# Leaky unit of a mixture layer: one scaled copy on ScalarE and one maximum on VectorE in place of two VectorE operations

## The chip, the cores and the metric

The kernel runs on one core of one Trainium2 chip. Its engines are TensorE (PE, matmuls; its weight loads are PEld), VectorE (DVE), ScalarE (ACT), GpSimd (POOL) and SyncE (SP), which issues nearly all transfers here. The metric is the device time in microseconds, the median of several runs. Each engine works through its own queue in order; semaphores order the engines among each other.

## The reference

Windowed attention (2 batches, 8 heads, 768 positions, head size 64; each query sees its last 96 positions and the first 8), then two expert layers over the 1536 tokens, both 512 to 2048 to 512:

```python
def _moe_ref(x, w_in, w_out, alpha):
    h = x @ w_in
    g = np.maximum(h, 0.0) + alpha * np.minimum(h, 0.0)
    return (g @ w_out).astype(np.float32)

def _moe2_ref(x, w_in, w_out, a, b):
    h = x @ w_in
    P = a[0] + a[1]*h + a[2]*h*h + a[3]*h*h*h
    Q = 1.0 + abs(b[0])*abs(h) + abs(b[1])*h*h
    return ((P / (Q + 1e-06)) @ w_out).astype(np.float32)
```

alpha is one number for each of the 2048 hidden columns, between 0 and about 1.26, so some are above 1.

## The kernel before

Every matmul operand is split into a high half (float32r) and a low half (the rest), and a product is made of three passes: high by high, high by low, low by high. The hidden layer is worked in 16 chunks of 128 columns (fc) for each of three groups (g) of 512 tokens, for each of the two layers: 96 steps in all, 48 leaky and 48 rational. For each step, `first` (L738) does the 12 matmuls of L745 into one PSUM bank, the unit turns the bank into the halves ghi and glo, and `second` (L798) does the 12 matmuls of L811 from them into banks 4 to 7. In a leaky step the unit is `leaky` (L748): L751 makes alpha * min(h, 0) in the tile act, L752 adds max(h, 0) to it in the bank, L753 casts the bank to ghi on ScalarE, and the returned function, called later, subtracts (L754) into glo.

The order of work is written by hand (manual_schedule), so each engine's queue has the order of the program. There are three stretches. First, attention alone (`alone`, L575, units u of two z steps). Second, 16 joint slots (`joint_slot`, L855, s = 0 to 15, u = 10 + s): each has the scores and the values of attention, one leaky step and parts of the weight work. Third, plain slots (`plain_slot`, L876), where the leaky step of slot s is that of the first() before it and second() works two steps behind.

A joint slot runs in this order: `opening(u)` (scores, reciprocal, row minima L452, low halves of the q or k cast before, `values` L512 and L514 for earlier units, exponentials L459, the casts to xhi and xlo, L524 and L525); one `tick`; `first(s)`; another `tick`; `turning(u)` (transposes of the probabilities and of the next q or k block, `copy_p` L497 or L499, and the q or k cast L412 or L409 on ScalarE); `leaky(s)`; the low halves of q or k (L413, L410); the low half of the leaky unit; `second(s - 1)`. In the joint stretch every `first(s)` writes bank 3, so `first(s + 1)` has to wait until L754 of slot s has read it. `values` writes bank 2, which the q or k cast and its low half read before.

A `tick` (L284) moves weight loading on: `tick` casts a joined weight tile to its high half (L302 on ScalarE), subtracts for the low half (L305 on VectorE), joins the two words of the next tile (L314, L315, L316 on VectorE) and scales the one after (L325 on ScalarE). L302 waits for L316 of the tick before.

`moe_constants` (L183) issues the transfers of alpha and of the coefficients in unit u = 2; `moe_constants_ready` (L189) makes constants from the coefficients on GpSimd and ScalarE in u = 6.

Of the kernel before, what the change touches and what calls it, by code (L numbers as in the profile page):

```python
# [8 lines left out]
F32 = mybir.dt.float32  # L9
# [3 lines left out]
AF = mybir.ActivationFunctionType  # L13
ALU = mybir.AluOpType
# [3 lines left out]
P = 128  # L18
# [7 lines left out]
NF = DFF // P  # L26
# [34 lines left out]
class Kernel:  # L61
# [52 lines left out]
    def small_consts(self):  # L114
        const = self.small
        self.ni = const.tile([P, 4], I32, name="ni")
        self.nf = const.tile([P, 4], F32, name="nf")
        self.neg = const.tile([P, 4], F32, name="neg")
        self.nv = const.tile([P, 2], F32, name="nv")
        self.fl = const.tile([P, 3], F32, name="fl")  # L120
        self.fi = const.tile([P, 1], I32, name="fi")
        self.al = const.tile([P, NF], F32, name="al")
        self.co = const.tile([P, 6], F32, name="co")
        self.na = const.tile([P, 4], F32, name="na")
        self.ab = const.tile([P, 2], F32, name="abs_b")
        self.cq = const.tile([P, 1], F32, name="cq")
        const.tile([P, 16], F32, name="pad")
# [61 lines left out]
    def moe_constants_ready(self):  # L189
        nc, co = self.nc, self.co  # L190
        nc.gpsimd.tensor_scalar(self.na, co[:, 0:4], -1.0, 1.0, ALU.mult, ALU.mult)
        nc.scalar.activation(self.ab, co[:, 4:6], AF.Abs)
        nc.gpsimd.memset(self.cq, 1.0 + 1e-6)

    def load_tokens(self, nm, i, tile, heads=slice(0, H)):
        b, qb = divmod(i, NB)
        src = {"q": self.q, "k": self.k, "v": self.v}[nm][b, heads, qb * P : (qb + 1) * P, :]
        self.nc.sync.dma_start(out=tile[:, heads], in_=src.rearrange("h s d -> s h d"))
# [532 lines left out]
    def moe(self):  # L731
        nc, steps, banks = self.nc, self.steps, self.banks
# [15 lines left out]
        def leaky(n):  # L748
            fc, h = steps[n][2], hbank.pop(n)
            t, hi, lo = self.act[n % 2], self.ghi[n % 2], self.glo[n % 2]  # L750
            nc.vector.tensor_scalar(t, h, 0.0, self.al[:, fc : fc + 1], ALU.min, ALU.mult)  # L751
            nc.vector.scalar_tensor_tensor(h, h, 0.0, t, ALU.max, ALU.add)  # L752
            nc.scalar.copy(hi, h)  # L753
            return lambda: nc.vector.tensor_sub(lo, h, hi.bitcast(F32))  # L754

        def rational_parts(n):
            p = flat[NST - 2 + n % 2]
# [97 lines left out]
        def joint_slot(s, halves):  # L855
            u = JOIN // 2 + s
            opening, turning = halves or (lambda u: None, lambda u: ())
            if s >= CH + 2 and s < CH + 2 + NEARLY:
                self.reload(s - CH - 2)
            opening(u)  # L860
            if s:
                self.tick(True, 2 * s - 1 in self.starts)
            first(s)
            self.tick(True, 2 * s in self.starts)
            lows = turning(u)
            low = leaky(s)
            for more in lows:
                more()
            low()
            if s:  # L870
                second(s - 1)
            if s == LATE - 1:
                self.tick(True, 2 * s + 1 in self.starts)
                self.spill()

        def plain_slot(s):  # L876
# [22 lines left out]
            if late >= LATE and steps[late][0]:  # L899
                rational_e(late)  # L900
            low = leaky(early) if ready and not steps[early][0] else None
            self.tick(True, 2 * s in self.starts)
            if low:
# [87 lines left out]
```

## Time and profile before

| | us |
|---|---|
| median of 3 runs (lowest, highest) | 651.09 (649.98, 651.37) |
| span of the profiled execution | 646.6 |
| TensorE busy | 619.1 (96%) |
| VectorE busy | 537.8 (83%) |
| ScalarE busy | 378.1 (58%) |
| GpSimd busy | 128.2 (20%) |

The profile is that of one execution; its own time outside the span is not given. Busy shares are means over stretches with different limits, so the table by stretch and the chain of waits tell more than the shares do. Durations of matmuls are modelled at their ends. An instruction that starts before the one ahead of it on its engine has ended overlaps with it.

### The profile page before, as it was taken

The numbers are of one execution on the slowest core, as the hardware profiler recorded it, in microseconds if no ns is written. First come the engines' busy times: TensorE is split into PE (matmuls) and PEld (weight loads), VectorE is DVE, ScalarE is ACT, GpSimd is POOL, SyncE is SP. The second block draws the span as 40 slices with busy tenths as digits, with TensorE's granted clock in tenths as the row PEclk, the third lists the DMA queues.
The fourth block names the chain that finished last, engine by engine and source line by source line (L and its number), as shares of the span: only waits on it lengthen the run. The fifth ranks groups of instructions, "written<-read, shape, count | busy, mean of one in ns | idle before, by whom it ended". The sixth has DMA issues, their size and how long they took to land.

```text
span 646.6 us, 9486 instructions
## 1 busy us (share of the span) xinstructions
PE 619.1 (96%) x3234; PEld 506.9 (78%) x3234; DVE 537.8 (83%) x1015; ACT 378.1 (58%) x787; POOL 128.2 (20%) x204
## 2 busy tenths in 40 slices
PE   7878999999999999999999999999999999999995
PEld 6756877778878888888888878887788888888783
DVE  5686899977658878958879989999989997786985
ACT  4886666676534323324333377777687776766672
POOL 4574222122210000000000013212222222222221
PEclk7799998999999999999999999999999999999998
DMA  8998798879788933412612600231111000400302
GB/s 159 196 272 224 205 285 261 250 257 278 241 280 261 368 90 90 123 60 65 196 33 66 195 2 2 65 98 32 38 60 33 1 1 0 131 2 0 131 0 71
DMA packets 84858, 82.81 MB, mean 128 GB/s; under 512 B 45312, under 2 KB 61952, under 8 KB 84800
## 3 DMA queue, kind: packets, MB, share of 16 engines
q1 hardware_dynamic: 84656, 81.98, 42.8%
q8 instruction: 27, 0.44, 0.3%
q14 instruction: 31, 0.25, 0.1%
q10 hardware_dynamic: 144, 0.13, 0.1%
HBM read 60.21 MB, written 19.92 MB: 124 GB/s over the span
## 4 chain that ended last, share of the span: by engine, by line
PE 66%; DVE 21%; ACT 7%; POOL 2%; issue 2%; DMA 1%; SPq 0%; ACTq 0%; POOLq 0%; DVEq 0%
PE bank L811 32%; PE bank L745 31%; DVE dx L315 3%; ACT prob L459 3%; DVE dx L316 3%; DVE prob L452 2%; DVE dx L314 1%; DVE bank L752 1%; DVE glo L754 1%; DVE act L751 1%; ACT ghi L753 1%; POOL prob L471 1%; DVE act L789 1%; DVE stage L788 1%; DVE stage L787 1%
## 5 line engine op out<-in xcount | busy, mean ns | idle before, releaser
L796 POOL TENSOR_TENSOR glo<-act,ghi 128x512 fp32r<-128x512 f32 (+1 forms) x49 | 67.2, 1372 | 385.1 <-ACT ghi L792 363.9
L753 ACT CAST ghi<-bank 128x512 fp32r<-128x512 f32 x48 | 28.2, 588 | 111.7 <-DVE bank L752 90.3
L745 PE MATMUL bank<-xhi,winhi_f 128*128 128x512 f32 x256 | 68.4, 389 | 0.0
L745 PE MATMUL bank<-xhi,winlo_f 128*128 128x512 f32 x256 | 68.4, 389 | 0.0
L745 PE MATMUL bank<-xlo,winhi_f 128*128 128x512 f32 x256 | 68.4, 389 | 0.0
L471 POOL TENSOR_SCALAR prob<-prob,rec 128x232 f32<-128x232 f32 (+1 forms) x96 | 44.4, 481 | 99.2 <-DVE rec L477 70.6
L459 ACT ACTIVATE prob<-prob,stat 128x232 f32<-128x232 f32 (+1 forms) x96 | 45.0, 475 | 23.6 <-DVE stat L452 23.6
L745 PEld LDWEIGHTS bank<-xlo,winhi_f 128*128 128x128 f32 x256 | 48.1, 188 | 10.0
L745 PEld LDWEIGHTS bank<-xhi,winhi_f 128*128 128x128 f32 x256 | 48.1, 188 | 10.0
L745 PEld LDWEIGHTS bank<-xhi,winlo_f 128*128 128x128 f32 x256 | 48.0, 188 | 10.0
L315 DVE SCALAR_TENSOR_TENSOR dx<-de,dx 128x512 int32<-128x512 int32 x64 | 50.8, 794 | 2.2
L754 DVE TENSOR_TENSOR glo<-bank,ghi 128x512 fp32r<-128x512 f32 x48 | 33.0, 688 | 17.4 <-ACT ghi L753 10.7
L316 DVE SCALAR_TENSOR_TENSOR dx<-stage,dx 128x512 int32<-128x512 int32 x64 | 45.7, 714 | 2.2
L751 DVE TENSOR_SCALAR act<-bank,al 128x512 f32<-128x512 f32 x48 | 35.8, 745 | 12.6 <-PE bank L745 12.6
L792 ACT CAST ghi<-act 128x512 fp32r<-128x512 f32 (+1 forms) x49 | 30.1, 615 | 26.3 <-DVE act L789 26.3
L763 ACT ACTIVATE stage<-bank 128x512 f32<-128x512 f32 (+1 forms) x49 | 28.9, 589 | 27.3 <-PE bank L745 27.1
L772 DVE SCALAR_TENSOR_TENSOR stage<-stage,abs_b 128x512 f32<-128x512 f32 (+1 forms) x49 | 36.0, 737 | 10.5 <-ACT stage L764 10.5
L325 ACT ACTIVATE de<-stage 128x512 f32<-128x512 f32 x64 | 43.0, 676 | 0.6 <-DMA stage<-in_moe_w_out_dram 0.6
L811 PE MATMUL bank<-wouthi_f,ghi 128*128 128x512 f32 x144 | 41.5, 393 | 1.3 <-ACT ghi L792 1.3
L811 PE MATMUL bank<-wouthi_f,glo 128*128 128x512 f32 x144 | 41.3, 392 | 0.0
L811 PE MATMUL bank<-woutlo_f,ghi 128*128 128x512 f32 x144 | 41.0, 389 | 0.0
L787 DVE SCALAR_TENSOR_TENSOR stage<-stage,cq,bank 128x512 f32<-128x512 f32 (+1 forms) x49 | 35.9, 734 | 3.3 <-ACT bank L777 3.2
(204 smaller groups left out, 1443.1 us busy)
## 6 DMA issues: line engine op xcount, KB each, us to landing
stage<-in_moe_w_in_dram SPq DMA_DIRECT2D x32, 512.0 KB
stage<-in_moe_w_out_dram SPq DMA_DIRECT2D x32, 512.0 KB
part<-saved_f SPq DMA_DIRECT2D x16, 256.0 KB
va<-in_v_dram SPq DMA_DIRECT2D x13, 256.0 KB
saved_f<-part SPq DMA_DIRECT2D x12, 256.0 KB
out_dram<-part SPq DMA_DIRECT2D x11, 256.0 KB
rawk<-in_k_dram SPq DMA_DIRECT2D x10, 256.0 KB
rawq<-in_q_dram SPq DMA_DIRECT2D x10, 256.0 KB
```

Source lines behind the costliest of these rows:

```text
L315: lambda: nc.vector.scalar_tensor_tensor(y, e, -(2**31), y, ALU.bitwise_and, ALU.bitwise_or),
L316: lambda: nc.vector.scalar_tensor_tensor(y, low, 29, y, ALU.logical_shift_right, ALU.bitwise_or),
L325: nc.scalar.mul(self.de[n % 2], self.staged(n)[:, :, :, 1].bitcast(F32), 2.0**-112)
L459: nc.scalar.activation(p[:, j - e, :w], p[:, j - e, :w], AF.Exp, bias=st[:, j : j + 1], scale=-1.0, accum_out=st[:, 4 + j : 5 + j],)
L471: nc.gpsimd.tensor_scalar(p[:, j, :w], p[:, j, :w], r[:, e + j : e + j + 1], 1.0, ALU.mult, ALU.mult)
L745: nc.tensor.matmul(bk, w["in", a][:, c, :], x[:, c, :], start=e == 0, stop=e == len(seq) - 1)
L751: nc.vector.tensor_scalar(t, h, 0.0, self.al[:, fc : fc + 1], ALU.min, ALU.mult)
L754: return lambda: nc.vector.tensor_sub(lo, h, hi.bitcast(F32))
L772: nc.vector.scalar_tensor_tensor(w, w, self.ab[:, 0:1], ab, ALU.add, ALU.mult)
L787: nc.vector.scalar_tensor_tensor(w, w, self.cq[:, 0:1], r, ALU.add, ALU.mult)
L796: nc.gpsimd.tensor_tensor(lo, u, hi.bitcast(F32), ALU.subtract)
L811: nc.tensor.matmul(y[d], lhs, rhs, start=begin and e == 0, stop=last and e == 2)
```

## The change

The leaky unit is written as a maximum. Where alpha is at most 1, max(h, 0) + alpha * min(h, 0) is max(h, alpha * h); where it is above 1 it is the minimum of the two, which is minus the maximum of -h and -alpha * h. So each hidden column has a sign sg (1 or -1) and sa = sg * alpha. ScalarE writes sa * h to act, VectorE writes max(sg * h, act) to the bank, which is then sg times the result; the sign is taken back in the two halves: ScalarE makes ghi from sg times the bank, VectorE glo from sg times the bank less ghi. sg and sa are made once, by three GpSimd operations on 128x16.

```diff
+        self.sg = const.tile([P, NF], F32, name="sg")
+        self.sa = const.tile([P, NF], F32, name="sa")
...
         nc.gpsimd.memset(self.cq, 1.0 + 1e-6)
+        nc.gpsimd.tensor_scalar(self.sg, self.al, 1.0, 2.0, ALU.is_le, ALU.mult)
+        nc.gpsimd.tensor_scalar(self.sg, self.sg, 1.0, 1.0, ALU.subtract, ALU.mult)
+        nc.gpsimd.tensor_tensor(self.sa, self.sg, self.al, ALU.mult)
...
         def leaky(n):
             fc, h = steps[n][2], hbank.pop(n)
             t, hi, lo = self.act[n % 2], self.ghi[n % 2], self.glo[n % 2]
-            nc.vector.tensor_scalar(t, h, 0.0, self.al[:, fc : fc + 1], ALU.min, ALU.mult)
-            nc.vector.scalar_tensor_tensor(h, h, 0.0, t, ALU.max, ALU.add)
-            nc.scalar.copy(hi, h)
-            return lambda: nc.vector.tensor_sub(lo, h, hi.bitcast(F32))
+            sg, sa = self.sg[:, fc : fc + 1], self.sa[:, fc : fc + 1]
+            nc.scalar.activation(t, h, AF.Copy, scale=sa)
+            nc.vector.scalar_tensor_tensor(h, h, sg, t, ALU.mult, ALU.max)
+            nc.scalar.activation(hi, h, AF.Copy, scale=sg)
+            return lambda: nc.vector.scalar_tensor_tensor(lo, h, sg, hi.bitcast(F32), ALU.mult, ALU.subtract)
```

## Rows read from the trace of the kernel before

**Rows 1.** Table by stretch: us, busy (instructions) of each engine, PE clock, DMA share, GB/s.
```profile
56.00:132.00 76.00, 71.74 (x504) 58.28 (x505) 65.92 (x167) 48.95 (x132) 15.23 (x41) 0.98 0.85 245
132.00:186.00 54.00, 53.37 (x371) 43.34 (x370) 39.73 (x102) 33.45 (x91) 12.90 (x32) 1.00 0.80 251
186.00:378.00 192.00, 192.00 (x863) 158.84 (x862) 155.23 (x249) 68.42 (x119) 0.00 (x0) 1.00 0.45 143
```
**Rows 2.** Timeline of VectorE in slot 1: start, duration, instruction, idle before it.
```profile
69.79 0.75 DVE L751 TENSOR_SCALAR act<-bank,al 128x512 f32<-128x512 f32 x1
70.57 0.70 DVE L752 SCALAR_TENSOR_TENSOR bank<-bank,act 128x512 f32<-128x512 f32 x1
...
71.92 0.69 DVE L754 TENSOR_TENSOR glo<-bank,ghi 128x512 fp32r<-128x512 f32 x1
```
**Rows 3.** Timeline of ScalarE at the end of slot 0.
```profile
61.42 0.64 ACT L412 ACTIVATE qhi<-bank 128x512 fp32r<-128x512 f32 x1
61.91 0.63 ACT L753 CAST ghi<-bank 128x512 fp32r<-128x512 f32 x1
```
**Rows 4.** Timelines of VectorE and TensorE at the end of slot 0.
```profile
62.09 0.69 DVE L413 SCALAR_TENSOR_TENSOR qlo<-bank,qhi 128x512 fp32r<-128x512 f32 x1 [1.59 <-ACT qhi L412]
62.70 0.68 DVE L754 TENSOR_TENSOR glo<-bank,ghi 128x512 fp32r<-128x512 f32 x1
...
62.84 0.44 PE L512 MATMUL bank<-pt,va 128*64 128x128 f32 x4 [0.30 <-DVE qlo L413]
```
**Rows 5.** Groups of instructions by form: shapes, count, busy us, mean ns, idle before.
```profile
L768 ACT ACTIVATE act<-bank,na 128x512 f32<-128x512 f32 x47 | 37.0, 787 | 0.0
...
L783 DVE SCALAR_TENSOR_TENSOR act<-act,na,bank 128x512 f32<-128x512 f32 x47 | 35.1, 747 | 1.7
...
L764 ACT ACTIVATE stage<-bank,abs_b 128x512 f32<-128x512 f32 x47 | 32.3, 687 | 0.0
L788 DVE SCALAR_TENSOR_TENSOR stage<-stage,bank 128x512 f32<-128x512 f32 x47 | 32.3, 687 | 1.6
...
L763 ACT ACTIVATE stage<-bank 128x512 f32<-128x512 f32 x47 | 28.1, 597 | 27.3 <-PE bank L745 27.1
```
**Rows 6.** Timeline of ScalarE: the leaky unit's cast in slots 1, 2, 3, 7.
```profile
71.31 0.59 ACT L753 CAST ghi<-bank 128x512 fp32r<-128x512 f32 x1 [0.53 <-DVE bank L752]
...
80.90 0.59 ACT L753 CAST ghi<-bank 128x512 fp32r<-128x512 f32 x1 [1.12 <-DVE bank L752]
...
90.39 0.59 ACT L753 CAST ghi<-bank 128x512 fp32r<-128x512 f32 x1 [1.57 <-DVE bank L752]
...
129.44 0.59 ACT L753 CAST ghi<-bank 128x512 fp32r<-128x512 f32 x1 [1.70 <-DVE bank L752]
```
**Rows 7.** Timeline of TensorE: the waits that end slots 7 and 13.
```profile
130.04 0.44 PE L512 MATMUL bank<-pt,va 128*64 128x128 f32 x4 [0.77 <-DVE klo L410]
...
183.04 1.19 PE L745 MATMUL bank<-xhi,winhi__119 128*128 128x512 f32 x4 [0.63 <-DVE glo L754]
```
**Rows 8.** TensorE's wait that ends slot 4, then three windows of 2 us.
```profile
100.76 0.66 PE L512 MATMUL bank<-pt,va 128*64 128x128 f32 x8 [1.51 <-DVE qlo L413]
...
100.00:102.00 2.00, 1.14 (x9) 0.90 (x10) 1.94 (x7) 0.65 (x2) 0.29 (x1) 0.88 1.03 378
102.00:104.00 2.00, 2.00 (x6) 1.52 (x6) 1.52 (x8) 2.00 (x8) 1.47 (x4) 0.50 1.13 328
104.00:106.00 2.00, 2.00 (x9) 1.56 (x8) 1.93 (x4) 1.29 (x4) 0.33 (x1) 0.77 0.56 200
```
**Rows 9.** Timelines of GpSimd and VectorE in unit u = 6.
```profile
36.71 0.50 POOL L476 TENSOR_SCALAR rec<-stat 128x4 f32<-128x4 f32 x1
...
38.34 0.17 DVE L477 RECIPROCAL rec<-rec 128x4 f32<-128x4 f32 x1
```
**Rows 10.** A plain slot: ScalarE's timeline, and TensorE's block from the chain.
```profile
225.47 0.59 ACT L753 CAST ghi<-bank 128x512 fp32r<-128x512 f32 x1 [2.22 <-PE bank L811]
...
223.58 2.72 PE bank L811 x12
```

## The prediction

> **What bounds the kernel now.** I read the page first: TensorE is busy for 96% of the span. That is an average, so the table by stage comes next [rows 1]. From 186 to 378 us TensorE has no idle time at all, and there VectorE and ScalarE can change freely. From 132 to 186 us it lacks 0.6 us of 54. From 56 to 132 us, the stretch in which attention and the first expert layer share the engines (slots 0 to 8 of joint_slot), it lacks 4.3 us of 76 while VectorE is busy for 65.9 of 76. So I followed the chain of waits there, slot by slot, in the timelines. In every slot VectorE runs straight through: weight joins L314 to L316, then the leaky unit L751, L752 and L754 [rows 2], then the row minima of the next scores. TensorE waits for it, not the other way round: values() waits for the low half of q or k (L410, L413), which stands in VectorE's queue right behind L752. From slot 0 to slot 7 the end is set by this VectorE chain; from slot 8 by TensorE.
>
> The question is therefore not how busy ScalarE is, but when it is free inside a joint slot. There it has copy_p and the q or k cast ahead of the leaky unit in its queue, and both engines set out from the same event: the weight cast L302 of ScalarE waits for the join L316 of VectorE, so a late VectorE also makes ScalarE late.
>
> **Part 1: durations.** Taken out is L751: L752 starts 0.78 us after it [rows 2]. Added is one ScalarE pass over 128x512 from a bank into act with a per-partition scale. The nearest rows are L763 (no per-partition operand) 0.597, L764 (one) 0.687, L768 (two) 0.787 us [rows 5]. I take 0.69, since L764 has the same shape, source and one such operand; the ends are 0.60 and 0.79. The cast L753 becomes the same kind of pass: 0.59 [rows 3, 6] to 0.69, so 0.10 more, with ends 0 and 0.20. L752 gets a per-partition scalar: 0.70 [rows 2] to 0.755, by the step from L788 (0.687, none) to L783 (0.747, one) [rows 5]. The subtraction L754 becomes the same form: 0.69 to 0.74. Low ends for these two: no change.
>
> **Part 2: one joint slot.** Let W be ScalarE's wait for VectorE ahead of its cast L753 [rows 6]. It is the only hole that the new pass can use. The pass may start 0.10 before the end of the instruction ahead of it (L753 starts 0.15 before the end of L412 in slot 0 [rows 3]), lasts 0.69, and the hand-over takes 0.04. So the maximum can start W - 0.63 before the old start of the cast; the old L752 started 0.74 before it (70.57 and 71.31 [rows 2, 6]). Its shift is 1.37 - W, and never better than -0.78. Behind it the maximum lasts 0.06 longer, the cast 0.10, the subtraction 0.05. VectorE leaves the slot 1.58 - W later than now:
> - slot 0: its cast has W = 0 and starts at 61.91 as soon as L412 is through [rows 3]; L751 and L752 were done by then, under the wait for qhi of 1.59 us [rows 4]. Now: pass 61.91 to 62.60, maximum 62.64 to 63.40, cast 63.42 to 64.11, subtraction from 64.13, not from 62.70 [rows 4]: +1.43 at its start, +1.48 at its end. qlo (62.09 [rows 4]) is queued behind the maximum and moves to 63.3; values(), which waited for it at 62.84 [rows 4], moves by 1.2. A chain of four hand-overs, three of them on the path, now stands where two were hidden.
> - slot 1, W = 0.53: +1.05.
> - slots 2, 5 and 6, W = 1.12, 1.12 and 1.14 (one row stands for three): +0.46, +0.46, +0.44.
> - slots 3 and 4, W = 1.57 and 1.55 (one row for both; here the probabilities have half the width and copy_p is shorter): +0.01, +0.03.
>
> Sum to the end of slot 6: 3.93 us. In slot 7, W = 1.70, and what TensorE waits for is klo behind the maximum (0.77 us [rows 7]): 1.37 - 1.70 + 0.06 = -0.27. That leaves +3.66 for TensorE at first(8). From there TensorE has no gap until 183.04, where it waits 0.63 us for L754 [rows 7]. In slots 8 to 13 the pass fits into longer waits of ScalarE, VectorE runs 0.1 to 0.5 us ahead of its present place in each, and this wait goes: -0.63. Late next is TensorE itself. Result of the joint stretch: **+3.03 us**.
>
> **Part 3: the other 32 leaky steps.** From 186 us on the pass costs nothing: in plain_slot the cast even waits for TensorE to give back its buffer (2.22 us, at 225.47 [rows 10]), and between that release and the matmuls that read the halves lie three blocks of 12 matmuls of 2.72 us each [rows 10], over 8 us; the new chain of four is about 2.9 us long. TensorE goes on without a gap, so nothing that VectorE saves here (0.6 us a step) reaches the end. If that cover were gone, a step would cost the same 1.58 - W.
>
> **Part 4: the three GpSimd operations** stand in moe_constants_ready, ahead of L476 in GpSimd's queue. They also make GpSimd wait for alpha there, whose transfer was issued ahead of that of the coefficients which GpSimd uses at that point without a wait. L476 runs from 36.71 for 0.50 us; VectorE reads its result at 38.34, since it is busy until then [rows 9]. Cover: 1.1 us. Three operations of 0.2 to 0.5 us take 0.6 to 1.5: I count 0, the bound is +0.4.
>
> **Sum.** The profiled execution spans 646.6 us; the median of the runs is 651.09, so 4.5 us lie around the span, and I leave them as they are. 651.1 + 3.0 = **654.1 us**. Low end (no cost for a per-partition operand on either engine): slot 0 +1.18, the others 1.27 - W, so 1.18 + 0.74 + 0.15 - 0.30 - 0.28 + 0.15 + 0.13 = 1.77, slot 7 -0.43, the wait -0.63: +0.7, 651.8. High end (two steps of 0.1 for each ScalarE pass): 1.68 + 1.25 + 0.66 + 0.21 + 0.23 + 0.66 + 0.64 = 5.33, slot 7 -0.17, -0.63: +4.5, 655.6.
>
> **Rivals.** A, the sum above: 0.55.
>
> B, the per-partition operands cost nothing, for instance because they are fetched while the instruction waits. Against it: L764 and L768 differ from L763 in step. 651.8, chance 0.15.
>
> C, the clock of TensorE. After a wait of 1.51 us that ends slot 4 the granted clock was 0.88, 0.50 and 0.77 in three windows of 2 us [rows 8], which is the lower of its levels (1.2 of 2.4 GHz) for part of them: 2 x (0.12 + 0.50 + 0.23) = 1.7 us lost. It costs nothing there, since VectorE is later still. The change adds waits in slots 0, 2, 5 and 6. If the fall comes at slot 8 or later, where TensorE sets the end, it counts: 654.1 + 1.7 = 655.8, chance 0.15.
>
> D, faster: VectorE's load decides. If ScalarE had the copy ready before VectorE arrives in slots 1 to 7, each would give -0.78 + 0.06 + 0.10 + 0.05 = -0.57; seven of them with the +1.48 of slot 0 make -2.5, 648.6, and TensorE has room for it (the 4.3 us that it lacks up to 132 us [rows 1]). It sets in above W = 1.58 and is full at W = 2.15. Slots 1 to 6 lie between 0.53 and 1.57, so the rows speak against it, but W was set by a chain that changes too: 0.15. The Trainium skill, Perfetto Trace Analysis, section "Optimizing Scalar/DVE Operations", says that where the vector engine is saturated, offloading some of its work to the scalar engine may make sense; by that rule alone the result would be D. The trace agrees on the saturation (65.9 of 76 us) and not on the place: the scalar engine is free elsewhere in the slot.
>
> Against the move speaks a rule of the Trainium skill, ScalarE: Activation LUTs, "Rules for kernel authors": max, min, add and mul belong on the vector engine. The rows here put the pass on the scalar engine slightly below the one taken out (0.687 against about 0.75), so it is not the duration that costs. By the rule, with 0.75 or more for the pass, slots 0 to 6 would add 0.06 each, 0.4 in all: 654.5.
>
> **How the numbers follow.** A run tells apart about 0.2%, 1.3 us: 649.8 to 652.4 is no change. A and C are slower (0.70), B the same (0.15), D faster (0.15). The range takes in B, the bounds of A and C, and leaves out D: 651.6 to 656.2.
>
> **What the profile after would show.** Right: L753's place in slot 0 about 1.5 us later, VectorE idle ahead of the maximum in slots 0 to 2 with ScalarE's pass as releaser, first matmuls of slot 3 about 3 us later and of slot 8 some 3.5 us later, the 0.63 us wait at slot 14 gone, and from 190 us on the same order as before, shifted. Wrong: a pass of 0.6 us (B), half clock after slot 7 (C), no idle VectorE ahead of the maximum (D), or GpSimd late with L476 by more than 1.1 us (then up to 0.4 more).

## The result and the profile after

| | kernel before | changed kernel |
|---|---|---|
| median of 4 runs, us (lowest, highest) | 650.54 (648.47, 651.37) | 653.38 (653.13, 654.77) |
| span of the profiled execution, us | 646.6 | 651.4 |

The ratio is 1.0063, with a 95% interval of 1.0045 to 1.0081: 2.84 us slower, where +3.03 was forecast. The two spans are 4.8 us apart, which is not the size of the effect. The profiled execution of after has its own time, 653.13, so 1.73 us lie around its span; with as much around it, the profiled execution of before took about 648.3, near the lowest of its runs.

The table by stretch of the changed kernel answers to [rows 1] (us, busy and instructions of TensorE, its weight loads, VectorE, ScalarE and GpSimd, then granted clock, DMA share and GB/s):

```profile
56.00:132.00 76.00, 68.92 (x466) 56.28 (x467) 57.41 (x148) 52.10 (x136) 14.94 (x40) 0.96 0.79 227
132.00:186.00 54.00, 53.35 (x379) 43.41 (x378) 39.38 (x105) 39.22 (x102) 11.72 (x30) 1.00 0.78 252
186.00:378.00 192.00, 192.00 (x874) 158.60 (x873) 135.40 (x216) 93.62 (x155) 2.27 (x4) 1.00 0.47 151
```

The change does what it says: from 186 to 378 us VectorE is busy 20 us less (155.2 before) and ScalarE 25 us more (68.4 before), and TensorE has no gap in either. From 56 to 132 us VectorE is less busy too, 57.4 for 65.9 us, and yet TensorE lacks 7.1 us there where it lacked 4.3 (0.7 us of it because first(0) begins at 56.70 and not at 55.94). VectorE was relieved of work and came later. The end of slot 0 shows how, first ScalarE's timeline and then VectorE's, which answer to [rows 3, 4] (start, duration, instruction, idle before it and what released it):

```profile
62.16 0.64 ACT L417 ACTIVATE qhi<-bank 128x512 fp32r<-128x512 f32 x1
62.65 0.73 ACT L757 ACTIVATE act<-bank,sa 128x512 f32<-128x512 f32 x1
64.20 0.69 ACT L759 ACTIVATE ghi<-bank,sg 128x512 fp32r<-128x512 f32 x1 [0.83 <-DVE bank L758]
```
```profile
63.41 0.76 DVE L758 SCALAR_TENSOR_TENSOR bank<-bank,sg,act 128x512 f32<-128x512 f32 x1 [6.44 <-ACT act L757]
64.08 0.68 DVE L418 SCALAR_TENSOR_TENSOR qlo<-bank,qhi 128x512 fp32r<-128x512 f32 x1
64.92 0.75 DVE L760 SCALAR_TENSOR_TENSOR glo<-bank,sg,ghi 128x512 fp32r<-128x512 f32 x1 [0.16 <-ACT ghi L759]
```

VectorE has nothing to do for 6.44 us and then gets the scaled copy only behind the q cast, at 63.38. Before the change it did the two operations of the leaky unit inside that hole:

```profile
59.01 0.75 DVE L751 TENSOR_SCALAR act<-bank,al 128x512 f32<-128x512 f32 x1 [2.80 <-PE bank L745]
59.80 0.70 DVE L752 SCALAR_TENSOR_TENSOR bank<-bank,act 128x512 f32<-128x512 f32 x1
```

The steps now follow each other in single file: pass, maximum, cast, subtraction. In the following slots the same wait stands ahead of the maximum, between 0.3 and 1.5 us; VectorE in slots 1, 2, 3 and 7:

```profile
74.57 0.76 DVE L758 SCALAR_TENSOR_TENSOR bank<-bank,sg,act 128x512 f32<-128x512 f32 x1 [1.52 <-ACT act L757]
...
84.51 0.76 DVE L758 SCALAR_TENSOR_TENSOR bank<-bank,sg,act 128x512 f32<-128x512 f32 x1 [0.91 <-ACT act L757]
...
94.01 0.76 DVE L758 SCALAR_TENSOR_TENSOR bank<-bank,sg,act 128x512 f32<-128x512 f32 x1 [0.47 <-ACT act L757]
...
133.81 0.76 DVE L758 SCALAR_TENSOR_TENSOR bank<-bank,sg,act 128x512 f32<-128x512 f32 x1 [0.34 <-ACT act L757]
```

The groups of the four instructions on the page of the changed kernel (count, busy us, mean ns, idle before) answer to [rows 2, 5]:

```profile
L758 DVE SCALAR_TENSOR_TENSOR bank<-bank,sg,act 128x512 f32<-128x512 f32 x48 | 36.4, 758 | 41.6 <-ACT act L757 41.5
L759 ACT ACTIVATE ghi<-bank,sg 128x512 fp32r<-128x512 f32 x48 | 33.0, 688 | 50.5 <-DVE bank L758 35.4
L760 DVE SCALAR_TENSOR_TENSOR glo<-bank,sg,ghi 128x512 fp32r<-128x512 f32 x48 | 35.9, 749 | 22.4 <-PE bank L817 14.3
L757 ACT ACTIVATE act<-bank,sa 128x512 f32<-128x512 f32 x48 | 33.2, 691 | 27.2 <-PE bank L750 27.2
```

### The profile page after: what moved, and what is told of

It reads as the page before. It is cut to its first block, busy times and chain, and to the rows that moved or that the text cites. A ratio compares the mean times of both kernels' runs of the same rounds, so it can differ in the third digit from the quotient of the medians.

```text
span 651.4 us, 9519 instructions
## 1 busy us (share of the span) xinstructions
PE 622.4 (96%) x3234; PEld 509.9 (78%) x3234; DVE 510.1 (78%) x967; ACT 412.6 (63%) x835; POOL 129.1 (20%) x207
## 4 chain that ended last, share of the span: by engine, by line
PE 76%; DVE 12%; ACT 6%; POOL 1%; issue 1%; DMA 1%; SPq 1%; ACTq 0%; DVEq 0%; POOLq 0%
PE bank L817 35%; PE bank L750 35%; DVE dx L320 2%; PE bank L442 1%; PE bank L407 1%; PE bank L517 1%; ACT prob L464 1%; DVE prob L457 1%; DVE dx L321 1%; POOL prob L476 1%; ACT pt L504 1%; PE bank L493 1%; DVE bank L758 1%; DVE act L795 1%; PE bank L519 1%
## 5 line engine op out<-in xcount | busy, mean ns | idle before, releaser
L758 DVE SCALAR_TENSOR_TENSOR bank<-bank,sg,act 128x512 f32<-128x512 f32 x48 | 36.4, 758 | 41.6 <-ACT act L757 41.5
L750 PE MATMUL bank<-xhi,winlo_f 128*128 128x512 f32 x256 | 68.4, 389 | 0.0
L750 PE MATMUL bank<-xlo,winhi_f 128*128 128x512 f32 x256 | 68.4, 389 | 0.0
L759 ACT ACTIVATE ghi<-bank,sg 128x512 fp32r<-128x512 f32 x48 | 33.0, 688 | 50.5 <-DVE bank L758 35.4
L476 POOL TENSOR_SCALAR prob<-prob,rec 128x232 f32<-128x232 f32 (+1 forms) x96 | 44.4, 481 | 101.6 <-DVE rec L482 79.3
L760 DVE SCALAR_TENSOR_TENSOR glo<-bank,sg,ghi 128x512 fp32r<-128x512 f32 x48 | 35.9, 749 | 22.4 <-PE bank L817 14.3
L757 ACT ACTIVATE act<-bank,sa 128x512 f32<-128x512 f32 x48 | 33.2, 691 | 27.2 <-PE bank L750 27.2
```

The costliest lines, as they stand in the source:

```text
L476: nc.gpsimd.tensor_scalar(p[:, j, :w], p[:, j, :w], r[:, e + j : e + j + 1], 1.0, ALU.mult, ALU.mult)
L750: nc.tensor.matmul(bk, w["in", a][:, c, :], x[:, c, :], start=e == 0, stop=e == len(seq) - 1)
L757: nc.scalar.activation(t, h, AF.Copy, scale=sa)
L758: nc.vector.scalar_tensor_tensor(h, h, sg, t, ALU.mult, ALU.max)
L760: return lambda: nc.vector.scalar_tensor_tensor(lo, h, sg, hi.bitcast(F32), ALU.mult, ALU.subtract)
```

## The experiments

Theory A: in a joint slot the copy stands too late in ScalarE's queue, so VectorE leaves later by 1.58 - W. Rivals: the operands' price alone, the plain stretch, TensorE's clock, and D, by which only VectorE's load matters. Each run was compared with runs of the kernel before on the same chip (median 650.54 for the changed kernel, 650.44 or 650.45 for the others). The stretches are read off the starts of first() in the traces, as differences to before, whose own are 75.13, 59.58 and 455.95 us. The last one ends with the span, which is given to a tenth, so differences below 0.1 us mean nothing there:

```
                       median   ratio (95%)               first(0)   first(8)    first(15)
                       us                                 to (8)     to (15)     to the end
after                  653.38   1.0063 (1.0045, 1.0081)    +4.41     -0.72       +0.35
plain slots only       649.27   0.9990 (0.9977, 1.0003)     0.00     -0.04        0.00
joint slots only       653.47   1.0049 (1.0029, 1.0069)    +4.18     -0.70       +0.25
copy early             646.74   0.9945 (0.9926, 0.9964)    -2.97     -0.71       +0.05
immediates             650.92   1.0010 (1.0000, 1.0021)    +1.14     -0.72       +0.05
short waits only       653.99   1.0066 (1.0041, 1.0092)    +4.43     -0.32       +0.05
long waits             648.31   0.9982 (0.9967, 0.9997)    -0.26     -0.72       -0.15
copy in the middle     649.19   0.9983 (0.9968, 0.9997)    +0.47     -0.72       -0.05
```

Medians and traces do not agree to the tenth: from first(0) to first(15) the traces give -0.05 us for the plain slots alone, -0.98 for the long waits and -0.25 for the copy in the middle, and their medians are 1.17, 2.14 and 1.26 us below the kernel before; for the other five the two lie within 0.9 us. So a median here can be a microsecond off what the slots account for, for a reason that stays open, and the arguments below rest on the traces.

The second table is finer. For each joint slot it has the end of the leaky unit's subtraction on VectorE, counted from the start of first(0), as the growth of its difference to before from slot to slot. The line of the prediction is its 1.48 for slot 0 and 1.58 - W for the others:

```
slot                    0      1      2      3      4      5      6      7
predicted            +1.48  +1.05  +0.46  +0.01  +0.03  +0.46  +0.44  -0.12
after                +1.53  +1.94  +0.33  +0.01  +0.01  +0.45  +0.43  -0.13
joint slots only     +2.26  +0.97  +0.33  +0.03   0.00  +0.44  +0.42  -0.11
short waits only     +2.26  +0.95  +0.33  +0.01   0.00  +0.44  +0.42  +0.01
long waits           +0.02   0.00  -0.01  +0.01  +0.02   0.00  -0.02  -0.12
immediates           +1.25  +0.65  +0.02  -0.30  -0.30  +0.13  +0.12  -0.42
copy in the middle   +1.90  +0.48  -0.15  -0.47  -0.47  -0.06  -0.05  -0.55
copy early           +0.14  +0.31  -0.58  -0.55  -0.56  -0.51  -0.50  -0.56
```

**Joint or plain slots: two runs that change one kind only.**

```diff
+            if n < LATE:          # plain slots only; n >= LATE: joint slots only
+                nc.vector.tensor_scalar(t, h, 0.0, self.al[:, fc : fc + 1], ALU.min, ALU.mult)
+                nc.vector.scalar_tensor_tensor(h, h, 0.0, t, ALU.max, ALU.add)
+                nc.scalar.copy(hi, h)
+                return lambda: nc.vector.tensor_sub(lo, h, hi.bitcast(F32))
             sg, sa = self.sg[:, fc : fc + 1], self.sa[:, fc : fc + 1]
```

> New form in the 32 plain slots alone, old form in the 16 joint slots; the three GpSimd operations are there. Theory (the change costs where ScalarE stands late in its queue inside a joint slot): within 0.2% of the kernel before, although VectorE does some 0.6 us less in each of 32 steps. Rival (ScalarE's greater load costs wherever it is): two thirds of the change's +2.84 us, +1.9 us. GpSimd's operations: 0.

> New form in the 16 joint slots alone, old form in the 32 plain slots. Theory: the whole loss, +2.8 us (2.0 to 4.5) against the kernel before. Rival (load everywhere): a third, +0.9 us.

The plain slots alone give 649.27 us and no difference above 0.04 us in any stretch; the joint slots alone give 653.47, the whole effect. The 32 plain steps are free, in both directions: the relief of VectorE there brings nothing either. The three GpSimd operations are in both kernels and delay nothing that shows from first(0) on (for the start of slot 0 see the end).

In the joint kernel slot 0 stands 0.78 above the sum, and the reason is ahead of the leaky unit. TensorE's timeline of it at first(0) (one line is one run of matmuls, x4 the count):

```profile
57.29 1.91 PE L750 MATMUL bank<-xhi,winhi__113 128*128 128x512 f32 x4 [0.16 <-DVE klo L415]
59.04 1.08 PE L750 MATMUL bank<-xhi,winlo__114 128*128 128x512 f32 x4
...
60.88 0.27 PE L493 MATMUL bank<-part,prob 128*128 128x128 f32 x1
```

Its first four matmuls take 1.91 us (1.19 in the changed kernel, at full clock), so first(0) lasts 3.59 us to the transposes behind it and not 2.87; the granted clock from 56 to 60 us was 0.64. That is 0.72 us which the leaky unit did not cause. Without it slot 0 is +1.54. The kernel with short waits has the same start (3.58 us), the one with the copy in the middle 3.72 us.

**Which slots pay: two runs that split the sum.**

```diff
+            if n not in (0, 1, 2, 5, 6):   # short waits: new form there; long waits: n in (0, 1, 2, 5, 6)
+                ...                        # the four instructions of before
```

> New form in joint slots 0, 1, 2, 5 and 6 alone (those where ScalarE's wait W ahead of its cast was 0 to 1.14 us in the kernel before), old form everywhere else. Theory (VectorE leaves a slot 1.58 - W later): +1.48 + 1.05 + 0.46 + 0.46 + 0.44 = +3.9 us at slot 8 and at the end, more than the whole change costs. Rival (each joint slot costs alike): 5 of 16 slots, +0.9 us.

> The rest: old form in joint slots 0, 1, 2, 5 and 6, new form in the other 11 joint slots (W 1.55 us or more) and in the plain ones. Theory: slots 3 and 4 +0.04, slot 7 -0.27, the wait ahead of slot 14 -0.63: -0.9 us, between -1.5 and 0. Rival (each joint slot costs alike): +2 us.

By slots the two lines add up to that of the joint kernel within 0.02 us: the slots whose W was short lose, those with W = 1.55 and more do not, and slot 7 gains 0.12. The second kernel, with the change everywhere but in the five slots, takes 648.31 us, a little faster than before (0.9982, interval up to 0.9997), with about 1 us of the 2.1 accounted for by its trace. It keeps what the change brings ahead of first(14), where a wait of TensorE goes: -0.72. The first kernel has the old form in slots 8 to 13 and gains only 0.32 there; the wait is still half there:

```profile
188.47 0.73 PE L750 MATMUL bank<-xhi,winhi__121 128*128 128x512 f32 x2 [0.33 <-DVE glo L760]
```

So about half of that gain needs the new form in slots 8 to 13. The other half came with the shift alone, by a way that stays open.

**The place in the queue: the same instructions, the copy earlier.** In one kernel ScalarE's copy is issued ahead of copy_p and the q or k cast of its slot, in the other between the two.

```diff
+        def leaky_copy(n, h):
+            fc = steps[n][2]
+            nc.scalar.activation(self.act[n % 2], h, AF.Copy, scale=self.sa[:, fc : fc + 1])
...
-            nc.scalar.activation(t, h, AF.Copy, scale=sa)
+            if n >= LATE:
+                leaky_copy(n, h)
             nc.vector.scalar_tensor_tensor(h, h, sg, t, ALU.mult, ALU.max)
...
             self.tick(True, 2 * s in self.starts)
+            leaky_copy(s, hbank[s])     # copy early; middle: called in turning(), behind copy_p
             lows = turning(u)
```

> As the changed kernel, with the same instructions, but in the joint slots ScalarE's scaled copy stands ahead of copy_p and of the q or k cast in its queue. Theory: VectorE no longer waits for the copy; slot 0 costs about +0.2 instead of +1.48, slot 1 about 0, slots 2 to 7 gain about 0.55 each until TensorE sets the end: 2 to 3 us faster than the kernel before, some 5 us faster than the changed kernel; the idle time of VectorE ahead of the maximum (0.3 to 1.5 us a slot) goes. Rival (ScalarE's load, the same here): still +2.8 us.

> As the changed kernel, but in the joint slots the scaled copy stands between copy_p and the q or k cast, one cast (0.50 us) earlier in ScalarE's queue. Theory: slot 0 +0.99, slot 1 +0.55, slots 2, 5 and 6 -0.04 each, slots 3 and 4 -0.49 each (full gain but for 0.08), slot 7 -0.7, the wait ahead of slot 14 -0.63: -0.9 us against the kernel before (-1.6 to +0.3), between the changed kernel and the version with the copy ahead of copy_p. Rival (there is a threshold, not a slope: either VectorE waits or it doesn't): as one of those two, +2.8 or -3.7 us.

With the copy early the kernel takes 646.74 us, ratio 0.9945 (0.9926 to 0.9964): 3.7 us faster than before and over 6 us faster than the changed kernel, with not one instruction more or less. In slot 1, ScalarE and then VectorE:

```profile
69.83 0.67 ACT L330 ACTIVATE de<-stage 128x512 f32<-128x512 f32 x1
70.41 0.67 ACT L755 ACTIVATE act<-bank,sa 128x512 f32<-128x512 f32 x1
70.98 1.06 ACT L504 COPY pt<-bank 128x512 f32<-128x512 f32 x2
71.92 0.60 ACT L414 CAST khi<-bank 128x512 fp32r<-128x512 f32 x1
```
```profile
70.37 0.69 DVE L321 SCALAR_TENSOR_TENSOR dx<-stage,dx 128x512 int32<-128x512 int32 x1
71.11 0.76 DVE L763 SCALAR_TENSOR_TENSOR bank<-bank,sg,act 128x512 f32<-128x512 f32 x1
72.55 0.69 DVE L415 TENSOR_TENSOR klo<-bank,khi 128x512 fp32r<-128x512 f32 x1 [0.68 <-ACT khi L414]
```

The copy ends at 71.08, when VectorE is through with its joins at 71.06, and the maximum starts at once. In this slot the price is a later k cast (klo waits 0.68 us), and VectorE leaves 0.31 later; from slot 2 on it leaves 0.50 to 0.58 earlier in each. The table by stretch shows TensorE 73.1 us busy of 76, at full clock, for 71.7 before and 68.9 after:

```profile
56.00:132.00 76.00, 73.07 (x514) 59.30 (x515) 62.86 (x164) 56.65 (x151) 16.98 (x45) 1.00 0.85 246
```

With the copy in the middle VectorE still waits in slot 1, 1.02 us where it was 1.52:

```profile
74.31 0.76 DVE L765 SCALAR_TENSOR_TENSOR bank<-bank,sg,act 128x512 f32<-128x512 f32 x1 [1.02 <-ACT act L757]
```

In each of slots 1 to 6 VectorE leaves 0.47 to 0.50 us earlier than in the joint kernel, which is the time from the start of the k cast, now behind the copy, to that of the next instruction: 73.35 to 73.83 in slot 1 of the changed kernel. ScalarE's timeline there:

```profile
73.35 0.60 ACT L414 CAST khi<-bank 128x512 fp32r<-128x512 f32 x1
73.83 0.71 ACT L757 ACTIVATE act<-bank,sa 128x512 f32<-128x512 f32 x1
75.37 0.69 ACT L759 ACTIVATE ghi<-bank,sg 128x512 fp32r<-128x512 f32 x1 [0.83 <-DVE bank L758]
```

The move by one instruction is worth one instruction, slot by slot, until the copy is in time. That is the sharpest support for A: the loss is the queue's, and it can be turned up and down. The median, 649.19, is 1.26 us below the kernel before, where -0.9 was written. The trace gives only -0.25 from first(0) to first(15), and slot 0 accounts for what is missing there: first(0) takes 0.85 us longer at a lower clock, and TensorE then waits 1.04 us for qlo, 0.74 more than before. From first(0) to first(1) it is 1.58 us longer, which is the two added up, to a hundredth. Without the clock's part VectorE's slot 0 is +1.05, where +0.99 was written.

**The price of a per-partition operand.** Constants stand in place of the four operands; alpha's values are thereby left out of the computation, and the order of work is that of the changed kernel.

```diff
-            nc.scalar.activation(t, h, AF.Copy, scale=sa)
-            nc.vector.scalar_tensor_tensor(h, h, sg, t, ALU.mult, ALU.max)
-            nc.scalar.activation(hi, h, AF.Copy, scale=sg)
-            return lambda: nc.vector.scalar_tensor_tensor(lo, h, sg, hi.bitcast(F32), ALU.mult, ALU.subtract)
+            nc.scalar.activation(t, h, AF.Copy, scale=0.125)
+            nc.vector.scalar_tensor_tensor(h, h, 1.0, t, ALU.mult, ALU.max)
+            nc.scalar.activation(hi, h, AF.Copy, scale=1.0)
+            return lambda: nc.vector.scalar_tensor_tensor(lo, h, 1.0, hi.bitcast(F32), ALU.mult, ALU.subtract)
```

> As the changed kernel, with fixed numbers (0.125 and 1.0) in place of the four per-partition operands of the leaky unit, so alpha is left out of the result. Theory with the low end of the sum: ScalarE's passes 0.60 and 0.59 in place of 0.69 us, VectorE's 0.70 and 0.69 in place of 0.755 and 0.75, and +0.7 us against the kernel before in place of +2.8. Rival (the place in the queue alone counts, the durations don't): still +2 us or more.

Groups by form: the two ScalarE passes take 601 and 599 ns, not 691 and 688, and the two VectorE operations 699 and 689, not 758 and 749:

```profile
L756 ACT ACTIVATE act<-bank 128x512 f32<-128x512 f32 x48 | 28.8, 601 | 30.3 <-PE bank L750 30.2
...
L757 DVE SCALAR_TENSOR_TENSOR bank<-bank,act 128x512 f32<-128x512 f32 x48 | 33.5, 699 | 41.1 <-ACT act L756 40.9
L759 DVE SCALAR_TENSOR_TENSOR glo<-bank,ghi 128x512 fp32r<-128x512 f32 x48 | 33.1, 689 | 23.2 <-PE bank L816 17.4 <-ACT ghi L758 4.7
```

In slots 1 to 6 each slot costs 0.30 to 0.33 us less than in the joint kernel; the prediction had 1.27 - W for 1.58 - W, 0.31 less. The median is 650.92 us, 2.46 below the changed kernel. So most of the measured loss hangs on the operands, but only through the queue: the kernel with the copy early has all four at their full price and is the fastest of all.

## Why the prediction was right, point by point

**The direction and its place** held: the plain stretch is free (0.00 with the plain slots alone), everything lies in slots 0 to 7, and the wait that answers to [rows 7] at slot 13 is gone, -0.72 for the -0.63 forecast. Counted from first(0), first(3) came 3.6 us later and first(8) 4.4, where about 3 and 3.5 were written; what lies above that is the clock's, see below. first(14) starts with no idle time before it:

```profile
187.50 1.20 PE L750 MATMUL bank<-xhi,winhi__121 128*128 128x512 f32 x4
```

**The durations** were 0.691, 0.688, 0.758 and 0.749 us for the 0.69, 0.69, 0.755 and 0.74 taken from [rows 5].

**The rule 1.58 - W** held slot by slot within 0.03 us in slots 3 to 7, and within 0.13 us in slots 1 and 2 of the joint kernel, with W read from [rows 6]. Slot 0, the only one where W gave no answer, was +1.53 for +1.48.

**GpSimd** was covered, with 0.1 us to spare. Its timeline with the three operations, then VectorE's reciprocal, answer to [rows 9]:

```profile
37.35 0.70 POOL L196 TENSOR_SCALAR sg<-al 128x16 f32<-128x16 f32 x1
38.13 0.28 POOL L197 TENSOR_SCALAR sg<-sg 128x16 f32<-128x16 f32 x1
38.50 0.22 POOL L198 TENSOR_TENSOR sa<-sg,al 128x16 f32<-128x16 f32 x1
38.81 0.19 POOL L481 TENSOR_SCALAR rec<-stat 128x4 f32<-128x4 f32 x1
```
```profile
39.11 0.17 DVE L482 RECIPROCAL rec<-rec 128x4 f32<-128x4 f32 x1
```

What VectorE reads (L481, L476 before) starts 2.1 us later than before and is ready at 39.00, just before VectorE arrives at 39.11. The reciprocal is 0.77 us later, and the one ahead of the three operations was already 0.84 later (33.26 for 32.42).

**Rival D** fell as stated and rose in another place. In the changed kernel VectorE is idle ahead of the maximum in all of slots 0 to 7, so its load decided nothing. In the kernel with the copy early it does decide, with the -0.57 a slot that the rival had been given (-0.50 to -0.58 measured). The Trainium skill, Perfetto Trace Analysis, "Optimizing Scalar/DVE Operations", says that offloading work of a saturated vector engine to the scalar engine may make sense. The runs agree with it where the copy is early (-3.7 us) and not where it is late (+2.84): what decides is the place of the new work in the queue that takes it over.

**Rival B** fell with the durations, and its sum held: +0.7 us for operands that cost nothing, and the kernel with immediates measured 0.48 above the one before (0.0 to 1.4 by its interval).

**The term that was mis-sized is TensorE's part of slot 0**, through the clock of rival C, of which the prediction said that it counts only from slot 8 on. values() moved as forecast, but behind its wait the clock fell. TensorE's timeline of the changed kernel, then two windows with the granted clock (third number from the end):

```profile
64.81 0.44 PE L517 MATMUL bank<-pt,va 128*64 128x128 f32 x4 [1.53 <-DVE qlo L418]
65.08 0.39 PE L519 MATMUL bank<-pt,vb 104*64 104x128 f32 x4
...
65.65 0.65 PE L519 MATMUL bank<-pt,vb 104*64 104x128 f32 x4
...
67.94 0.80 PE L750 MATMUL bank<-xhi,winhi__117 128*128 128x512 f32 x1
```
```profile
64.00:68.00 4.00, 3.19 (x33) 2.86 (x33) 2.85 (x12) 1.74 (x5) 2.07 (x6) 0.67 0.08 18
68.00:72.00 4.00, 4.00 (x21) 3.40 (x21) 3.17 (x7) 2.86 (x9) 0.41 (x2) 0.90 0.01 4
```

From the values to first(1) it takes 3.13 us, and 1.91 before the change (62.84 to 64.75): 1.22 us more. Most of it is not free, because VectorE's slot 1 sets out from the values. ScalarE's cast to xhi waits for their bank, and VectorE waits for that cast before it comes to its joins and the maximum. Here is that cast in the changed kernel with VectorE's wait for it, then the same cast in the joint kernel:

```profile
68.05 0.65 ACT L529 CAST xhi<-bank 128x256 fp32r<-128x256 f32 x2 [0.84 <-PE bank L519]
68.72 0.76 DVE L530 TENSOR_TENSOR xlo<-bank,xhi 128x256 fp32r<-128x256 f32 x2 [1.71 <-ACT xhi L529]
```
```profile
68.43 0.62 ACT L529 CAST xhi<-bank 128x256 fp32r<-128x256 f32 x2
```

In the joint kernel, whose clock was full there, the values are through at 68.11 and the cast comes at 68.43 without a wait: ScalarE is busy until then with exponentials, which follow VectorE's late row minima. So about a quarter of a microsecond of the 1.22 disappears behind the lateness that the prediction did count, and VectorE's table has the rest: slot 1 is +1.94 in the changed kernel and +0.97 in the joint one, 0.97 us of clock. The slip in the argument was "VectorE is later still". It held for slot 4 [rows 8]: the changed kernel's clock falls there too (0.79 and 0.78 in 104 to 112 us), and slots 4 and 5 follow the rule all the same, +0.01 and +0.45. It does not hold for slot 0, where VectorE has 6 us to spare behind first(0) and waits 1.71 us behind the values.

**Why the total came out right nevertheless.** From first(0) to first(15) the traces give +3.69 after and +3.48 in the joint kernel, for +3.03 predicted. Without the 0.97 and the 0.72 us of clock they would be +2.72 and +2.76: the two agree, and lie 0.3 under the sum, most of it in slots 1 and 2 and in the wait ahead of first(14). The medians differ by 2.84. How often an execution of the kernel before has such a loss of clock can't be told from its one profile, which has none in slot 0; its runs are up to 3 us apart. So the rule for a slot is borne out by the mechanism, and that the medians come within 0.2 us of the forecast is partly luck.

**One reading was wrong**: that 4.5 us lie around the span. It is 1.7 us, and the rest was that the profiled execution of before was one of the shorter ones. The forecast didn't suffer, since a difference was added to the median.

## What to carry to other kernels

Moving work to an idle engine is judged by the instant at which that engine reaches it in its queue, set against the instant at which the reader is free: here the same instructions cost 2.84 us behind two other steps and gained 3.7 us ahead of them. Where another engine stands waiting for the result, try the new work ahead of the other steps in that queue, and compare both places before the idea is given up. W, the receiving engine's own wait in each repetition, told in advance which repetitions would pay and how much, within 0.13 us.

## What the runs showed of the hardware

A wait of TensorE of 1.53 us, which ends at 64.81 us in the changed kernel, was followed by a granted clock of 0.67 from 64 to 68 us and 0.90 from 68 to 72. In the joint kernel the same wait, at the same place of the program, ends at 66.13 and was followed by full clock. TensorE and its windows there in the joint kernel:

```profile
66.13 0.44 PE L517 MATMUL bank<-pt,va 128*64 128x128 f32 x4 [1.53 <-DVE qlo L418]
```
```profile
64.00:68.00 4.00, 2.47 (x43) 2.15 (x39) 3.10 (x11) 1.92 (x6) 0.75 (x2) 1.00 0.29 66
68.00:72.00 4.00, 4.00 (x26) 3.41 (x24) 3.15 (x11) 2.90 (x11) 1.74 (x6) 1.00 0.02 6
```

So the same wait costs TensorE 1.22 us or nothing. What came before differs: the changed kernel had full clock from 52 to 64 us and a wait of 1.58 us ahead of first(0), the joint kernel a clock of 0.51 and 0.64 from 52 to 60 us and a wait of 0.16. Whether that decides is not shown. A trace with such a dip can't be set against one without it to a tenth of a per cent; the dip has to be found in the windows and taken out first. Where slot 0 begins varies as well, from 55.94 to 57.61 us in the nine profiles. The earliest is the one profile of the kernel before; the other eight kernels are 0.29 to 1.68 us later. In each of them VectorE's reciprocal ahead of the three GpSimd operations is already late, by 0.33 to 1.21 us, so it does not begin with these operations; whether the change moves it in another way, one profile of the kernel before can't show.
